# Attention in 64x32 tiles of TensorE, even heads above, odd heads below, with products in the free half

## The chip, the cores and the metric

The kernel runs on one core of one Trainium2 chip. The metric is the device time of one execution in microseconds (us). A core has a matrix engine (TensorE, in the views PE for its matmuls and PEld for its weight loads), a vector engine (VectorE, DVE), a scalar engine (ScalarE, ACT), GpSimd (POOL) and a queue engine that here only issues DMAs (SyncE, SP). The engines run side by side, each through its own instructions in program order, and wait for each other by semaphores. SBUF is the working memory, of 128 partitions; PSUM is the memory into which TensorE writes, eight banks of 128 x 512 fp32 values.

## The reference: what is computed

Four layers of multi-query attention, in which two sets of weights alternate (A, B, A, B), on one sequence of S = 2048 rows of D = 512, with H = 32 query heads of width 16 and one key and one value head for all of them:

```python
q = (x @ wq).reshape(B, S, H, Dh).transpose(0, 2, 1, 3)
k = x @ wk
v = x @ wv
scores = einsum("bhqd,bkd->bhqk", q, k) * Dh ** -0.5
o = einsum("bhqk,bkd->bhqd", softmax(scores), v)
x = x + o.transpose(0, 2, 1, 3).reshape(B, S, H * Dh) @ wo
```

where the `x` on the right of the first three lines is the layer norm of the layer's input. All is fp32. Of a layer the scores are the bulk: 32 x 2048 x 2048 exponentials, 4 x 134 million in all.

## The kernel before, in words

**Tiling.** Queries are cut into NB = 4 blocks of 512, the 32 heads into NM = 4 groups of 8. A *pair* (lines 486 on) is a layer, a block and a group: 64 pairs. The 8 heads of a pair are taken in two halves of four, even and odd (`odd`). For one half and one chunk of 128 keys, a *unit*, `scores` (line 566) makes two score tiles `st` of 128 keys x 1024 (two heads x 512 queries) in PSUM. Each is two matmuls side by side: a weight of 64 rows x 128 keys (`kop`) and 512 moving columns of queries (`qt`), one in rows 0 to 63 of the array and one in rows 64 to 127. The 64 rows hold 16 dimensions four times, since key and query are each kept as a sum of two fp16 numbers. Three `st` tiles (NST = 3, six banks) take turns.

**Exponentials.** ScalarE turns an `st` into probabilities `pt` in SBUF (line 598, fp32, eight buffers). No maximum is subtracted; a check of ranges sets a flag, and a general path that is not taken here would do the work again. For 274 of the 4,096 tiles (letter V) VectorE does it instead, in `v_exp` (line 605): one operation that reads PSUM (line 609), two on the bits of the result (611, 613) and four of a polynomial (614 to 617), each reading what the one before wrote.

**Probabilities times values.** `pv` (line 619) is four matmuls of a unit (line 636) with fp32 weights of 128 keys x 32 columns (`vop`: 16 of values, 16 of ones, so that numerators and denominators come together) and 512 moving columns of `pt`, side by side in the four column strips of the array. An fp32 matmul is two passes in the records. They add up in a bank `acc` over the 16 chunks. `merge` (line 505) then moves numerators and denominators of even and odd heads from `acc` into two sums (lines 515, 518). For a whole pair come a reciprocal of 512 columns (line 537), a shuffle that brings denominators to their numerators (538), a multiplication (539) and the split into two fp16 parts (540, 541).

**Products.** Queries, keys, values and outputs are fp16 products in three terms (`mm3`, lines 297 to 299: high x high, high x low, low x high), as full 128x128 matmuls of 512 columns: 12 for one tile of 512 columns, and 64 + 16 + 64 such tiles in all. Around them stand layer norm (`normed`, line 311), transposes (338), splits, and squared lengths for the check (414, 416). They run as generators, one piece for each letter M, m or l, in whichever of the two `acc` banks is idle. Query tiles go to DRAM and come back in the layout of `qt` by eight DMAs for each pair (line 454).

**Order.** A string `ORDER` (line 57) fixes the order of everything after the front part: S and V for a score tile (exponential on ScalarE or VectorE), P and Q for `pv` of the first or second waiting unit, M, m and l for background work, v for one operation of a VectorE exponential, d for one of a division. The loop of line 673 walks through it; each engine's program follows. Scores come in runs of two or four, then probabilities, then background, so TensorE goes from one tile shape to another some thousands of times.

Of the kernel before, what the change touches and what calls it, by code (L numbers as in the profile page):

```python
# [31 lines left out]
W = 2  # L32
NST = 3
NPT = 8
# [14 lines left out]
LEAD4 = 0.01353416811725628  # L49
C0, C1, C2, C3 = 37.67975997924805, 23.0539493560791, 12.31057357788086, -0.15702559053897858  # L50
LOG2E = 1.4426950408889634

# [4 lines left out]
ORDER = (  # L57
    "mSSSMMMSSSPPSSMSSPPSSMMSSSPPSSMMSSPSSPPSSSPPSSMMSSSMMSPSSPSSMPSmSPSSPPSSSPmPSMSSPSSPPSSSMPSPSSSPMSSPSSPM"
    "SSPSmSMMSSPSMMSSPSSPSSMPSmSPPSSSPPSSPmSSPMSSPSSMSPSSPPSMSSSPPSSSPMSSPSmSMMMSSSMPSSPSSPPSMSSPmSSPPSSSPPmS"
    "SSMPSSPSSPMSSPSSMSPSSPPSSMSSPPmSSMSSMMSSPMSSPSSPSSMPSmSPPSSVPvSmSSPSPvSSvSmQSQvSQvSSmSQvSVQSSmPvSSvSPSSQ"  # L60
    "mmmQSSSQlvSMvMSvSQvSSMdMSSQQSSSPdPSSPdSdSPdPSVSPvSSvMvSSPvQvSSMvMSSVQvSMSSSPPSvSPvSSQvQvSSSQvQdSSPSSPPSS"
    "VPSvMvSSvSMMvMSSSPvQSvSQdSSdQdPdSSVPSMSvSMvSSvPPvSSSvQvQSSdMMSSSQPSSdPdVSMSPSSSmPvPvSvSQSvSMvMSSQvQVSSMv"
    "MSSSvQvQvSSPSSQvQSvSSQddQdSSPSSPPdSdVSPSvMvSSMSvSPQvSSvMMSSvSQlQddSSQVSPvSSvSPvPSSMvMSSvSQvQSSMVSQvSSvSQ"
    "vPvSSPvSSQvQSVSQvSSvMSSPvPSvSSQvQvSSMSSQQSVSPSSMvSSvPvPSvSSQvQvSSMdMSSSQQSSPdSSdPdPdVSSMvMvSSvSPPvSSvQSv"
    "SMMSSQVSQvSSvSPvPSSPvSSQvQvSSSMMVSQvSSvSQvPvSSPvSSQvQSVSMvMSSSQvPvSSPvSSvQQvSVSQSvMSSPmSSPvQvSSSvMMSSvQQ"
    "vSSdSQQSSMdSSdPdPdSVSPvSvSMSSvPPvSSvQSvSQVSQvSSvSMvMSSPvPSSSQvQvSSMVSQvSSvSQvPvSSPvSSQvQSVSQvSSvSPvPvSSS"
    "vQQvSMSVSQmSSSPPSSSQvQmSvSSvMQSSQvSSQvMSSQSSQvMSSQSdSPPSSPdSSdPdSdMSSPPmSSMVSPvSSvSMvMMSSSPQSSQSvSQvMSSQ"
    "QmvSSVMMSvSSQvPvSSvPSvSQvQSSVQvSMvSvSSPvPSvSMSSQvQSVSPSSSPvPvSvSMvMSSSQvQvSSQdSSQPSSdSPdPddSSMMSVSPmvSSv"
    "SPvPvSSMvSSQvQSVSQvSvSMSSvPPSSSvQQvSSvMSVMSQvSSvSQvPvSSPvSSQvQSVSMvMSSSvQvPSvSPvSSQvQSVSQvSSvSMvMSSPmPSS"
    "SQQSSQvSSvQmQvSSSMQSSPdPSSSPPdSdSMSPSdSPdMSSPSVPvSMSSPSmSMvMvSSQvSSMvMSSQQSSSQvQSVMSQvSSSlvPvPSvSQvSSMvQ"  # L70
    "SVSQvSvSSPvPvSSMvSSQvQSVSPSSMvSSvPvPSvSSQvQvSSMSSQdQSSPSSPdSdSPddPSVSPvSvSMvMSvSSPvQSvSQSVMSvMSSSQvPSSPv"
    "SSQvQvSSSMvMVSQvSSvSQvPvSSPvSSQvQSVSQvSSvMvMSSSPvPSSvQSvSQQSVSPSSMvSSvPvPSvSSQvQvSSQdSSQSSPdPdSSdMdMSVSP"
    "vSSvMSSPvPSvSQvSSQvQSSVQvSMSSvPmSSPvQSvSSMvMSSQvQSVSQvSvSSPvPvSSMvSSQvQSVSQvSvSMSSvPPvSSvQSvSMMSSQVSQvSS"
    "vSPPSvSPvSSQvQSvSSQdQSSPSSdPdPddSSVMMSSvSPmvPvSSvMMSSvSQvQSVSQvSSvSMvMSSPvPSSSQvQvSSMVSQvSSvSQvPvSSPvSSQ"
    "vQSVSQvSSvMSSvPPvSSvSQvQSVSQvSSvSMvMSSPvPmSSSQQSSQSvSQvQmSSVQSvMSSPSSvPvSQvSSQvSSvQMSSQSdSPPSMSSPSSdPPSd"
    "SVPSMSSPvSmvSMvMSvSQvSSQvQSdSdMVSQvSSvSPvPvSSMSSQQSSvSQvQSSVQvSMSSPlmSSPSQlSQvSvSSQvSSmQvSSQvSVQmSSSvPvS"
    "PvSSvQmSQSvSSQvSSmQdPSSPSSPmlmSSPSSPlSdSdMdMdSSPPSVSPvSSvMvSSPvQvSSMSSQvQSSMVSQvSSvSPvPvSSMvSSQvQSVSQvSv"
    "SPvSSMvMSSPSSQvQSvSSQdQSSPSSPdPddSSdSMMVSPvSSvSPvPvSSQvSSMvMSSQSSQPSVSPvSvSPSSMvMSSvPSvSQvQVSSMvMSSSQvQv"
    "SSPvSSvQQvSSVQSvMSSQmvSvSPvPSvSSQvQSSQSSPddddddddddddddddddddPSSSPPSSMMSSPSSPPSSSMMSSPPSSMMSSSPPSSPSSMMS"
    "SPmSSPPSSMSSPPSSMSSPPSSMSSPPSSMSSPmPSSMSSPPSSSPPSSMSSPMSSPSMSSPmSSPPSSSPPmSSSMPSSPMSSSPPSSPMSSSPPSSMPSSS"  # L80
    "mMMMSSSMPSSPSSPSPMSVSPmvSSvSPvPSSQmSSQvSSvQSvSmSPSSPPmSSSPSPSPmSSPdSPSSPmSSPdSmmSPSSVPlvSSvSMvMSvSMMSSPS"
    "SQvQvSSSQdQddSSdPSSPPdSVSPSvMvSSvSPvQSvSMSvSQdQdSdSSPPSVSPvSvSSMvMSPSSSQvQvSSMvSSQQSVSPvSvSSPvPvSSMvSSQv"
    "QSVSQvSvSMvMSSSPvPSvSQSvSQQSVSPSSMvSSvPvPSvSMSvSQvQSdSSQQSSMdSdSPddPSVSPvSvSMSSPvPvSSQvSSQvQSSVQvSMSSvPm"
    "SSPvQSvSSMvMSSQvQSVSQvSvSSPvPvSSMvSSQvQSVSQvSvSMSSvPPvSSvQSvSMMSSQVSQvSSvSPPSvSPvSSQvQSvSSQdQSSPSSdPdPdd"
    "SSVMMSSvSPmvPvSSvMMSSvSQvQSVSQvSSvSMvMSSPvPSSSQvQvSSMVSQvSSvSQvPvSSPvSSQvQSVSQvSSvMSSvPPvSSvQSvSQVSQvSSv"
    "SMvMSSPvPmSSSQQSSQSvSQvQmSSVQSvMSSPSSvPvMSSQSSQvQvSSSMQSSvQMSSQdSmSPPSSSPPdSdSMddMSSMVSPvSSvSPvPvSSMSSQQ"
    "SSvQSvMSSQQlSSMVSPvSSvSPvPvSSMvSSQvQSVSPSSMvSSvPvPSvSSQvQvSSMSSQdQSSPSSPdPddSVSMMvSvSSPvPvSSQvSSMvMSSQdQ"
    "SVSPvSSvPSSMvMSSvPSvSQvQSSMVSQvSSvSQvPvSSPvSSQvQSVSQvSSvMSSPvPSvSSQvQvSSQSVPSSSPvPvSvSMMvSSQvSSvQQdSSSPP"
    "SdSMdMSSPddSVMSPSvSSPmvPvSSvMMSSvQSvSQQSVSQvSSvPSSPvQvSSSMvMSSQvQSVSQvSvSSPvPvSSMvSSQvQSVSQvSvSMSSvPPvSS"
    "vSQvQSVSQvSSvPSSPvSSMvMSSQlvQvSSSQdQSSPSdSPdPddSVSMMvSvSSPvPvSSMvMSSQSvSQQSVSQvSSvSPvPSSMvMSSvSQvQSSQVSQ"  # L90
    "vSSvSPvPvSSMvMSSSQvQSSMVSQvSSvSQvPvSSPvSSQvQSVSQvSSvPSSMvMSSvPSvSQvQSdSSQQSSPdSdSPddPSVSPvSSvMSSPvQSvSSM"
    "vMSvSQQSVSQvSSvMvMSSSPvPSSQSvSQQvSVSQSvMSSPmvSvSPvQSvSSQvQSSMVSPvSvSMSSvPPvSSvQSvSQVSQvSSvSMvMSSPPSvSSQv"
# [86 lines left out]
def fast_path(ctx, tc, x_in, weights, out, flag):  # L181
# [80 lines left out]
    def load_split(key, w):  # L262
# [3 lines left out]
        for c in range(NC + 2):  # L266
# [8 lines left out]
            if c:  # L275
                yield False
# [564 lines left out]
```

## Time and profile before

| | |
|---|---|
| median of 3 runs | 3643.64 us (3640.91 to 3644.29) |
| profiled execution, first to last instruction (span) | 3639.3 us |
| TensorE busy (matmuls) | 3575.5 us, 26,707 records |
| ScalarE busy | 3552.5 us |
| VectorE busy | 3084.4 us |
| first and last exponential on ScalarE | 36.13 us, 3619.19 us |
| mean granted TensorE clock | 0.996 of full speed |

The profile is of one execution of its own, and its page gives no time for it but the span; the median of the runs is 4.3 us above that span. In the views a group of instructions is given by line, engine, operation, what is written and read with partitions x elements and type, the count, then busy time in us and the mean of one in ns, then the engine's idle time just before and what ended it. A timeline row has start, length, engine and line, and merges like instructions that follow one another (x8). A busy engine need not be at its peak: the records of matmuls overlap, and a record also holds latency.

### The profile page before, as it was taken

Reading aid. Unit: us, or ns where it says so; the run is one execution under the profiler, and the core shown is the slowest. Engines: PE = TensorE matmul, PEld = TensorE weight load, DVE = VectorE, ACT = ScalarE, POOL = GpSimd, SP = SyncE. Lnnn points to the kernel's source line nnn. Section 1 sums busy time; section 2 is a strip of 40 time slices with the busy share of each in tenths; the row PEclk is TensorE's granted clock in tenths of the full one; section 3 lists DMA queues with packets and bytes.
Section 4 is the critical chain, followed back from the end, with each engine's and each line's share of the span. In section 5 each row is a group of like instructions: output and inputs, shape, how many; then the busy total and the mean of one; then the engine's idle time right before and its main releaser. Section 6 shows DMA issues by size and latency. Waiting matters only on the chain.

```text
span 3639.3 us, 63025 instructions
## 1 busy us (share of the span) xinstructions
PE 3575.5 (98%) x26707; PEld 925.5 (25%) x26707; DVE 3084.4 (85%) x3606; ACT 3552.5 (98%) x3828; POOL 116.8 (3%) x122
## 2 busy tenths in 40 slices
PE   7999999999999999999999999999999999999998
PEld 2222222222222222222222222222222222222221
DVE  4598989998578998988958889988986889899988
ACT  6999999999999999999999999999999999999997
POOL 1000000000000000000000000000000000000000
PEclk9999999999999999999999999999999999999999
DMA  2110100000010010101001000010101101010000
GB/s 89 41 53 13 47 11 29 21 30 30 24 50 21 24 36 13 41 19 36 24 30 45 15 29 25 18 42 18 47 7 36 47 16 36 21 36 13 23 20 13
DMA packets 94819, 108.11 MB, mean 30 GB/s; under 512 B 15936, under 2 KB 72256, under 8 KB 94528
## 3 DMA queue, kind: packets, MB, share of 16 engines
q1 hardware_dynamic: 94208, 102.95, 8.8%
q8 instruction: 211, 3.46, 0.4%
q0 software_dynamic: 320, 1.05, 0.1%
q14 instruction: 80, 0.66, 0.1%
HBM read 70.39 MB, written 33.55 MB: 29 GB/s over the span
## 4 chain that ended last, share of the span: by engine, by line
PE 86%; ACT 11%; DVE 2%; DMA 1%; issue 0%; SPq 0%; POOL 0%; ACTq 0%; DVEq 0%; POOLq 0%
PE acc L636 47%; PE st L581 27%; ACT pt L598 10%; PE qps L297 2%; PE ops L297 2%; PE qps L298 1%; PE qps L299 1%; PE ops L299 1%; PE ops L298 1%; ACT dpt L598 1%; PE tps L338 1%; PE kps L297 0%; DVE den L537 0%; PE kps L299 0%; PE kps L298 0%
## 5 line engine op out<-in xcount | busy, mean ns | idle before, releaser
L598 ACT ACTIVATE pt<-st 128x1024 f32<-128x1024 f32 x3548 | 3311.5, 1046 | 41.0 <-PE st L581 30.4
L636 PE MATMUL acc<-pt,vop 128*32 128x512 f32 x14192 | 1799.5, 601 | 0.1
L581 PE MATMUL st<-qt,kop 64*128 64x512 f16 x8192 | 1269.5, 382 | 30.8 <-DMA qt<-qs 9.7
L581 PEld LDWEIGHTS <-kop 64*128 64x128 f16 x8192 | 357.0, 94 | 1581.5 <-issue 1474.1
L636 PEld LDWEIGHTS acc<-pt,vop 128*32 128x32 f32 x14192 | 345.5, 108 | 704.8 <-issue 684.7
L609 DVE TENSOR_SCALAR e<-st 128x1024 int32<-128x1024 f32 x274 | 335.3, 1224 | 199.3 <-PE st L581 194.8
L617 DVE SCALAR_TENSOR_TENSOR dpt<-dpt,e 128x1024 f32<-128x1024 f32 x274 | 339.7, 1240 | 8.5
L615 DVE SCALAR_TENSOR_TENSOR dpt<-dpt,mant 128x1024 f32<-128x1024 f32 x274 | 338.9, 1237 | 7.1
L616 DVE SCALAR_TENSOR_TENSOR dpt<-dpt,mant 128x1024 f32<-128x1024 f32 x274 | 336.9, 1230 | 7.6
L614 DVE SCALAR_TENSOR_TENSOR dpt<-mant 128x1024 f32<-128x1024 f32 x274 | 336.4, 1228 | 0.0
L636 PE MATMUL acc<-dpt,vop 128*32 128x512 f32 x2192 | 290.8, 602 | 0.0
L598 ACT ACTIVATE dpt<-st 128x1024 f32<-128x1024 f32 x274 | 282.9, 1033 | 5.0 <-ACT pt L598 4.3
L537 DVE RECIPROCAL den<-den 128x512 f32<-128x512 f32 (+1 forms) x76 | 215.9, 2841 | 0.4
L613 DVE TENSOR_SCALAR e<-e 128x1024 int32<-128x1024 int32 x274 | 193.6, 707 | 7.9
L611 DVE TENSOR_SCALAR mant<-e 128x1024 int32<-128x1024 int32 x274 | 189.8, 693 | 8.2
L436 DVE SCALAR_TENSOR_TENSOR xt<-ops,xt 128x512 f32<-128x512 f32 x140 | 96.4, 688 | 79.0 <-PE ops L299 78.1
L403 POOL TENSOR_TENSOR sq<-qs 128x512 bf16<-128x512 f16 x64 | 66.8, 1043 | 1611.6 <-DVE qs L400 1611.6
L518 DVE SCALAR_TENSOR_TENSOR num<-acc,half,num 128x512 f32<-128x512 f32 x92 | 69.0, 750 | 56.6 <-PE acc L636 55.7
L297 PE MATMUL ops<-wo,ot 128*128 128x512 f16 x252 | 97.4, 386 | 3.7 <-DVE xt L436 3.7
L297 PE MATMUL qps<-xnT,wq 128*128 128x512 f16 x256 | 99.1, 387 | 1.4 <-DVE wq L269 0.7
L298 PE MATMUL qps<-xnT,wq 128*128 128x512 f16 x256 | 97.4, 380 | 0.6 <-DVE xnT L342 0.6
L299 PE MATMUL qps<-xnT,wq 128*128 128x512 f16 x256 | 97.3, 380 | 0.4 <-DVE wq L270 0.4
(99 smaller groups left out, 1383.2 us busy)
## 6 DMA issues: line engine op xcount, KB each, us to landing
qt<-qs SPq DMA_DIRECT2D x624, 64.0 KB, 2.2
qs<-qs SPq DMA_DIRECT2D x64, 256.0 KB, 2.2
xs<-xt SPq DMA_DIRECT2D x48, 256.0 KB, 2.0
xt<-xs SPq DMA_DIRECT2D x48, 256.0 KB, 3.4
xt<-in_A_x_dram SPq DMA_DIRECT2D x32, 256.0 KB, 3.5
out_dram<-xt SPq DMA_DIRECT2D x16, 256.0 KB, 2.1
wst<-in_A_wo_dram SPq DMA_DIRECT2D x8, 256.0 KB, 2.7
wst<-in_B_wq_dram SPq DMA_DIRECT2D x8, 256.0 KB, 2.7
```

Of the source, the lines that this page charges most:

```text
L297: PE.matmul(ps, a[0], b[0], start=first, stop=False)
L537: lambda c=c: V.reciprocal(den[:, c], den[:, c]),
L581: PE.matmul(st[:, k * 512:(k + 1) * 512], kop[l % 2][c // 4][r, (c % 4) * P:(c % 4 + 1) * P], qt[pr][r, 2 * half + odd], start=True, stop= ...
L598: e = nc.scalar.activation(pt, st, AF.Exp, scale=SCALE / UP / UP).ins
L609: V.tensor_scalar(e, st, SCALE / UP / UP * LOG2E * 2.0 ** 23, 127 * 2.0 ** 23, ALU.mult, ALU.add)
L611: lambda: V.tensor_scalar(mant.bitcast(I32), e, 0x7FFFFF, 0x3F800000, ALU.bitwise_and, ALU.bitwise_or),
L613: lambda: V.tensor_scalar(e, e, 0x7F800000, None, ALU.bitwise_and),
L614: lambda: V.scalar_tensor_tensor(p, mant, C3, mant, ALU.add, ALU.mult),
L615: lambda: V.scalar_tensor_tensor(p, p, C2, mant, ALU.add, ALU.mult),
L616: lambda: V.scalar_tensor_tensor(p, p, C1, mant, ALU.add, ALU.mult),
L617: lambda: V.scalar_tensor_tensor(p, p, C0, e.bitcast(F32), ALU.add, ALU.mult)])
L636: PE.matmul(acc[s][32 * j:32 * j + 32, :], v[l % 2][c // 4][:, c % 4, 16 * odd:16 * odd + 32], p_of[u, j % 2][:, (j // 2) * 512:(j // 2 + ...
```

## The change

Nearly all of the fast path is written anew; the arithmetic is the same but for the constants of the VectorE exponential.

- **One tile shape.** Scores, probabilities and most products run as 64x32 tiles: `both` issues up to two lists of operations, one for rows 0 to 63 and one for rows 64 to 127, each operation being four matmuls in the four column strips. A score tile (`score`) is now 64 keys x all 8 heads of the pair: upper rows and lower rows of the array give columns 0 to 511 and 512 to 1023, and the even heads come out on partitions 0 to 63, the odd ones on 64 to 127. `pv(0)` takes even heads in the upper rows, `pv(1)` odd heads in the lower, each with 64 keys x 32 weights and 256 columns, into a bank of its own (`acc[0]`, `acc[1]`).
- **Products in the other half.** A full product becomes 24 half products of 64 rows x (4 x 32) columns. A table `STEPS` gives each letter its upper and lower operation: a is even and odd probabilities, b two half products above and odd probabilities below, c the reverse, and so on; V is half a score tile for VectorE. All products use one bank, `beside`. F (transposes, squared lengths) and P (full products in the front and at the end) keep other shapes.
- **Buffers.** Two score tiles instead of three, a bank `by_v` for scores that VectorE reads, `beside`, and two for sums; 16 probability buffers instead of 8.
- **VectorE exponentials.** 378 instead of 274; two chains can be open, letters 0 and 1, and one is taken up to 24 tiles ahead of the others. The first operation is done in two halves of 512 columns (letter I).
- **Sums and divisions.** An `acc` is copied or added as a whole (letter G, 170 times instead of 312 merges). For a division DMAs gather the 8 rows of denominators into a tile of 128 x 32, VectorE inverts that, and DMAs by way of DRAM spread the result over 16 partitions for each head. The last pair keeps the old way.
- **Outputs** of a block start when all four groups of it are divided, instead of group by group. Splits of weights and norms are single operations (letter X), Y is a copy of one column, weights are loaded from SP's queue. The order string is new (14,484 letters, 3,718 of them S, 756 with half a score tile for VectorE).

The diff, cut to its core:

```diff
-W = 2
-NST = 3
-NPT = 8
+NST = 2
+NPT = 16
+AHEAD = 24
...
+STEPS = {"S": "SS", "a": "EO", "b": "NO", "c": "EN", "d": "MO", "e": "EM", "f": "VO", "g": "EV",
+         "h": "WO", "i": "EW", "j": "VM", "k": "MV", "l": "E-", "m": "-O", "n": "N-", "o": "-N",
+         "p": "M-", "q": "-M", "r": "V-", "s": "-V"}
...
-    vop = [[one.tile([P, 4, 48], F32, name=f"vop{i}_{b}") for b in range(NB)] for i in range(2)]
+    vop = [[one.tile([P, 8, 32], F32, name=f"vop{i}_{b}") for b in range(NB)] for i in range(2)]
...
+    def both(ops):
+        turn[0] += 1
+        for n in range(max(map(len, ops))):
+            for r in range(2):
+                if n >= len(ops[r]):
+                    continue
+                bank, o, w, x, start, stop = ops[r][n]
...
+                h = slice(64 * r, 64 * r + 64)
+                for j in range(4):
+                    PE.matmul(o[32 * j:32 * j + 32], w[j][h], x[j][h], start=start, stop=stop,
+                              skip_group_check=True, tile_position=(64 * r, 32 * j))
...
+    def moving(n, r):
+        g, c, h = halves[n]
...
+        k = kop[l % 2][c // 8][:, c % 8 * 64:c % 8 * 64 + 64]
+        q = qt[groups[g][0]]
+        return (cols(k) * 2, [q[:, 2 * h], q[:, 2 * h], q[:, 2 * h + 1], q[:, 2 * h + 1]], True, True)
...
-        for k in range(W):
-            r = slice(64 * k, 64 * k + 64)
-            PE.matmul(st[:, k * 512:(k + 1) * 512],
-                      kop[l % 2][c // 4][r, (c % 4) * P:(c % 4 + 1) * P],
-                      qt[pr][r, 2 * half + odd], start=True, stop=True)
+        both([[(("st", s, r), st[s][:, 512 * r:512 * r + 512]) + moving(n, r)] for r in range(2)])
...
-        for j in range(4):
-            v = vop4 if u in split and j % 2 == 0 else vop
-            PE.matmul(acc[s][32 * j:32 * j + 32, :],
-                      v[l % 2][c // 4][:, c % 4, 16 * odd:16 * odd + 32],
-                      p_of[u, j % 2][:, (j // 2) * 512:(j // 2 + 1) * 512],
+        v = vop[l % 2][c // 8][:, c % 8]
+        cs = slice(256 * n, 256 * n + 256)
+        x = [pts[:, i[j % 2], (j // 2) * 512 + 256 * n:(j // 2) * 512 + 256 * n + 256]
+             for j in range(4)]
...
+        return ("acc", odd), acc[odd][:, cs], [v] * 4, x, (c, n) == (2 * c0, 0), last
...
+    def step(what):
+        ops = [[], []]
+        for r, w in enumerate(STEPS[what]):
+            if w in "EO":
+                ops[r].append(pv(r))
+            if w in "VW":
+                ops[r].append(score_v(r))
+            for _ in range({"N": 2, "M": 1, "W": 1}.get(w, 0)):
+                ops[r].append(work.next_pe().step(r))
+        both(ops)
...
+    def divide(pr):
...
+        for j in range(4):
+            for odd, t in ((0, ev[32 * j + 16:32 * j + 17]), (1, od[32 * j:32 * j + 1])):
+                h = 32 * j + 16 * odd
+                SP.dma_start(den[h:h + 16], t.rearrange("o (p q) -> o p q", p=16))
...
+        def invert():
+            V.reciprocal(den, den)
+            SP.dma_start(rs.rearrange("h (p q) -> (h p) q", p=16), den)
+            for j in range(4):
+                SP.dma_start(ev[32 * j + 16:32 * j + 32], od[32 * j + 16:32 * j + 32])
...
+        def spread():
+            r.append(one.tile([P, BQ], F32, name="rec"))
+            for h in range(2 * NM):
+                SP.dma_start(r[0][16 * h:16 * h + 16], rs[h:h + 1].to_broadcast([16, BQ]))
```

1159 lines of the change are left out of this document (701 added, 458 removed).

## The prediction

> **What bounds the kernel now.** I read the page's busy shares first, then the chain that ended last, then the groups by line.
>
> ```profile
> span 3639.3 us, 63025 instructions
> PE 3575.5 (98%) x26707; PEld 925.5 (25%) x26707; DVE 3084.4 (85%) x3606; ACT 3552.5 (98%) x3828; POOL 116.8 (3%) x122
> PE 86%; ACT 11%; DVE 2%; DMA 1%; issue 0%; SPq 0%; POOL 0%; ACTq 0%; DVEq 0%; POOLq 0%
> L598 ACT ACTIVATE pt<-st 128x1024 f32<-128x1024 f32 x3548 | 3311.5, 1046 | 41.0 <-PE st L581 30.4
> L636 PE MATMUL acc<-pt,vop 128*32 128x512 f32 x14192 | 1799.5, 601 | 0.1
> L581 PE MATMUL st<-qt,kop 64*128 64x512 f16 x8192 | 1269.5, 382 | 30.8 <-DMA qt<-qs 9.7
> ```
>
> Two engines are at 98%, and the chain says which one leads: 86% of it is TensorE. Busy time doesn't say what TensorE does with it. The chain in order of time and TensorE's timeline do:
>
> ```profile
> 2000.54 1.85 PE acc L636 x16
> 2002.39 0.76 PE st L581 x6
> 2003.15 0.99 PE acc L636 x8
> 2004.14 0.32 PE st L581 x2
> ...
> 2012.05 0.39 PE L297 MATMUL ops<-wo,ot 128*128 128x512 f16 x1
> 2012.27 0.38 PE L298 MATMUL ops<-wo,ot 128*128 128x512 f16 x1
> 2012.49 0.38 PE L299 MATMUL ops<-wo,ot 128*128 128x512 f16 x1
> ```
>
> Full products start 0.22 us apart (0.216 over five), so 512 fp16 columns stream in 0.216. A score run of two matmuls (one pair, side by side) takes 0.32 and one of six 0.76: 0.22 for each pair and 0.10 once. A probability-value run of 8 takes 0.99 and of 16 1.85: 0.43 for each pass of four, and 0.13 once. So every run of one tile shape pays **0.10 to 0.13 us when the shape changes** (64x128 for scores, 128x32 for probabilities, 128x128 for products). In the order string score letters stand next to probability letters 2,710 times and background letters next to either 1,209 times, of which I take 800 to issue matmuls: 2,710 x 0.115 + 800 x 0.10 = 392 us. Streaming itself is 4,096 pairs x 0.216 = 885, 4,096 fours x 0.43 = 1,761, 144 products of 12 x 0.216 = 373, the small ones about 40: 3,059. With 36 before the first exponential and 20 after the last (rows below) TensorE needs 3,507.
>
> ```profile
> 36.13 1.02 ACT L598 ACTIVATE pt<-st 128x1024 f32<-128x1024 f32 x1 [11.16 <-PE st L581]
> 3611.76 7.43 ACT L598 ACTIVATE pt<-st 128x1024 f32<-128x1024 f32 x8
> ```
>
> Eight exponentials in 7.43 us with 1.03 for one give a spacing of 0.91. ScalarE needs 3,822 x 0.91 + 56 = 3,534. The span is 105 above that: the price of two engines that wait for each other in a fixed order. Times here are spans of the profiled execution; the median of the runs, 3643.64, is 4.3 above it.
>
> **The change part by part.** *Shapes.* Scores, probabilities and most products become 64x32 tiles, four across and two high. Streamed columns stay: a score tile is 8 matmuls of 512 columns at once (0.216), a probability step is two passes of 256 fp32 columns in each half (0.43), and a product takes half the array and so twice as many steps, in the half that a probability step leaves free. Counting the new string by its table: 3,718 S x 0.216 = 803; 4,913 steps with a probability pass (a to i, l, m) x 0.43 = 2,113; 1,154 short steps (j, k, p, q, r, s) x 0.216 = 249; 15 long ones 6. The 93 F (transposes, squared lengths) keep other shapes; I take 0.65 for each, a few short matmuls between two changes: 60 (twice that would still lie inside TensorE's slack below). Sum 3,234; the changes left are these excursions instead of some 3,500. Whether a change of type alone costs as much (scores are fp16, probabilities fp32) one place shows:
>
> ```profile
> 68.61 0.40 PE L414 MATMUL gps<-sq,bones 128*32 128x512 bf16 x4
> 68.84 0.38 PE L416 MATMUL gps<-ksq,bones 128*32 128x512 bf16 x1
> 68.84 1.23 PE L636 MATMUL acc<-pt,vop 128*32 128x512 f32 x8
> ```
>
> From bf16 to fp32 in the same 128x32 tiles the next pass starts 0.23 us after the last, no 0.1 added; and while one column tile still ran line 416, the others went on, so unequal halves needn't wait for each other. I take zero for a type change (less than nothing is excluded, since columns can't stream faster; the other end, 0.115, is a rival below).
>
> *Front and end.* The front is the same work in nearly the same order: 36, give or take 5. The end loses the early output products: all 12 products of four rows come behind the last division, through one bank, instead of 3. That is 36 more at 0.216, and these are not hidden: +8, and four combinations instead of two merges +1, waits for the one bank +3. So 32 instead of 20. TensorE needs 3,234 + 68 = **3,302**.
>
> *ScalarE.* 104 fewer exponentials: 3,718 x 0.91 + 68 = **3,451**.
>
> *VectorE* gets those 104 (274 to 378), so every one of its rows counts.
>
> ```profile
> L609 DVE TENSOR_SCALAR e<-st 128x1024 int32<-128x1024 f32 x274 | 335.3, 1224 | 199.3 <-PE st L581 194.8
> L617 DVE SCALAR_TENSOR_TENSOR dpt<-dpt,e 128x1024 f32<-128x1024 f32 x274 | 339.7, 1240 | 8.5
> L613 DVE TENSOR_SCALAR e<-e 128x1024 int32<-128x1024 int32 x274 | 193.6, 707 | 7.9
> L400 DVE TENSOR_SCALAR qs<-qps 128x512 f16<-128x512 f32 x64 | 43.7, 683 | 34.7 <-PE qps L299 19.8 <-issue 14.3
> L537 DVE RECIPROCAL den<-den 128x512 f32<-128x512 f32 x60 | 200.8, 3346 | 0.2
> L537 DVE RECIPROCAL den<-den 128x128 f32<-128x128 f32 x16 | 15.2, 948 | 0.1
> L538 DVE STREAM_SHUFFLE tmp<-den 128x512 f32<-128x512 f32 x60 | 44.2, 737 | 0.0
> L541 DVE TENSOR_TENSOR ot<-num,ot 128x512 f16<-128x512 f32 x60 | 41.9, 698 | 1.9
> L518 DVE SCALAR_TENSOR_TENSOR num<-acc,half,num 128x512 f32<-128x512 f32 x92 | 69.0, 750 | 56.6 <-PE acc L636 55.7
> ```
>
> Means aren't spacings on this engine:
>
> ```profile
> 274.22 1.22 DVE L615 SCALAR_TENSOR_TENSOR dpt<-dpt,mant 128x1024 f32<-128x1024 f32 x1
> 275.48 1.22 DVE L616 SCALAR_TENSOR_TENSOR dpt<-dpt,mant 128x1024 f32<-128x1024 f32 x1
> 276.62 0.68 DVE L436 SCALAR_TENSOR_TENSOR xt<-ops,xt 128x512 f32<-128x512 f32 x1
> 277.22 1.22 DVE L617 SCALAR_TENSOR_TENSOR dpt<-dpt,e 128x1024 f32<-128x1024 f32 x1
> ```
>
> Line 616 needs 615's result and starts 1.26 after it; 436 needs nothing of 616 and starts 1.14 after it, before it has ended. A stranger in between saves 0.12. The new order works two chains in turn and puts other work between, so that only 251 of the 2,268 chain operations that would pay it follow their own predecessor. Per exponential: two halves from PSUM 2 x 0.60, two integer steps 2 x 0.61, four 4 x 1.14: 6.98. 378 x 6.98 + 251 x 0.12 = 2,668. The sums give back: 312 merges of 0.745 become 170 evacuations of 0.66 (232 to 112). The reciprocal falls from 512 columns to 32 (by its two rows 6.2 ns a column, so about 0.3) and the shuffle goes; a division is now 388 in all (216 of it reciprocals, four more operations of 0.44 to 0.74), then 126. Of the 3,084 busy that leaves 393 for norms, splits and copies beside 2,071 of exponentials; a few copies go: 382. The 135 touches of one column 13. Sum **3,301**, and 45 at both ends where it has little: 3,346.
>
> *Queues.* Each of 63 divisions adds 21 DMAs to SP's queue (8 gather sums, 1 stores reciprocals, 4 move rows, 8 spread them), and weight loads move there from POOL's.
>
> ```profile
> 1999.80 2.30 SPq L454 DMA_DIRECT2D qt<-qs  x5
> qt<-qs SPq DMA_DIRECT2D x624, 64.0 KB, 2.2
> ```
>
> At 0.46 an issue that is 1,323 x 0.46 = 609 us more of SP's queue, under a fifth of the span; some wait for a landing (2.2) and hold the query loads behind them. A pair of head groups lasts some 54 us, and loads are issued ahead, which hides it: I take zero, and up to 60 in all if the cover goes.
>
> *New waits.* Two score tiles instead of three: the S that waits for an exponential holds back all TensorE steps behind it. A score for VectorE waits until its one bank is read; a product waits until VectorE has read the bank of the last one; each holds the queue in the same way. After the end of an exponential 0.22 of streaming and some 0.16 of latency (0.38 in the rows less 0.22) fit into the 0.91 of the other tile, unless a 0.43 step stands in front. Bounded by nothing and by 135 (now 105, a third more for the third engine); I take 60, since TensorE now has 150 to spare under ScalarE where it had 27.
>
> Sum: 3,451 + 60 = 3,511 of span, 4 around it: **3515 us**.
>
> **The rivals.** *The order locks three engines.* Priced as above and counted over any 200 S, TensorE needs 167 to 180, ScalarE 182, VectorE 175 to 184: no engine can absorb another's delay. Waits of 150 instead of 60 give 3,600. For it: now too 105 us are lost with only two engines tied. Against: 16 probability buffers instead of 8.
>
> *VectorE becomes the bound* (the other side). Place: the chains of the 378 exponentials. If the strangers between don't overlap, each operation costs its mean and 0.03: 756 x 0.71 + 756 x 0.74 + 1,512 x 1.26 + 633 = 3,634, with both ends **3,700**. It decides from a mean spacing of 1.22 for the long ones on; the rows above say 1.14 beside a stranger, so little speaks for it but the missing slack.
>
> *TensorE is handed too many instructions.* 64x32 tiles take 111,000 matmuls and as many loads, 223,000 instead of 53,414. It decides at (3,643 - 68) / 223,000 = 16 ns each.
>
> ```profile
> 148.62 0.38 PE L581 MATMUL st<-qt,kop 64*128 64x512 f16 x2
> 149.04 0.19 PEld L636 LDWEIGHTS acc<-pt,vop 128*32 128x32 f32 x8 [0.53 <-PE st L581]
> 149.07 0.64 PE L636 MATMUL acc<-pt,vop 128*32 128x512 f32 x4
> ...
> 2009.65 1.92 PE L636 MATMUL acc<-pt,vop 128*32 128x512 f32 x16
> 2011.51 0.61 PE L581 MATMUL st<-qt,kop 64*128 64x512 f16 x4
> ```
>
> After a wait 8 loads (each 0.11) and 4 matmuls start within 0.08 us: 7 ns each. The longest dense stretch has 32 in 1.86, 58 ns, but there the array sets the pace. Between 7 and 58 I take the burst; at 18 ns the time would be 4,080. [...]
>
> *The change doesn't do what it says:* a change of type drains the array too. S alternates with other steps some 7,300 times: + 840, 4,140. Only the place at 68.8 us speaks against it.
>
> **How the numbers follow.** Forecast 0.62 (3440 to 3600), locked order up to the old time 0.14, within 0.2% (about what a measurement of this kernel can tell from no change) 0.04, VectorE bound 0.07, instructions 0.08, type change 0.05. Low end: no waits and a spacing just under 0.91 (0.905). High end: 3660, which holds the first three, 0.80. Faster 0.76, same 0.04, slower 0.20.
>
> **What would show it.** ScalarE stays at 96% or more with about 3,718 exponentials; TensorE's share of the chain falls and ScalarE's grows; score and probability steps start 0.22 and 0.43 apart with no 0.1 between; VectorE is busy for 95% or more; the end takes about 32 us. Wrong would be: steps of eight matmuls at 0.3 or more (instructions or type), VectorE's long operations at 1.26 (its bound), or ScalarE idle before scores by several hundred us (locked order).

## The result, and the profile after

| | before | changed |
|---|---|---|
| median of 4 runs | 3643.09 us (3640.91 to 3644.29) | 4017.83 us (4014.05 to 4022.31) |
| ratio, 95% interval | | 1.103 (1.101 to 1.105) |
| span of the profiled execution | 3639.3 us | 4020.5 us |
| mean granted TensorE clock | 0.996 | 0.953 |

The forecast was 3515 us, faster, with a range of 3440 to 3660. The kernel became 10% slower. The page of the changed kernel, its busy shares, the chain that ended last by engine, and the group of ScalarE's exponentials:

```profile
span 4020.5 us, 236136 instructions
...
PE 3565.0 (89%) x111943; PEld 2278.3 (57%) x111943; DVE 3326.8 (83%) x4449; ACT 3457.8 (86%) x3724; POOL 151.9 (4%) x110
...
DVE 31%; PE 31%; SPq 16%; ACT 11%; DMA 7%; issue 3%; DVEq 0%; POOL 0%; ACTq 0%
...
L752 ACT ACTIVATE pt<-st 128x1024 f32<-128x1024 f32 x3718 | 3453.6, 1081 | 508.3 <-PE st L469 501.8
```

No engine is near 98% now, so no engine's work alone is the bound. The chain says what came in: 16% of it is SP's queue and 7% transfers, which had been 0 and 1%. ScalarE waits 502 us for scores, but that is only who was waited for last. The waits of the changed kernel (engine and line, what it waited for, then us in total, times, longest) show where it starts:

```profile
ACT pt L752 <- PE st L469: 501.8, 276, 10.6
DVE sum L917 <- DMA rec<-rs: 236.0, 60, 10.0
DVE den L899 <- DMA den<-sum: 201.2, 51, 6.1
PE by_v L469 <- DVE e L781: 165.5, 65, 9.7
...
PE by_v L469 <- DMA qt<-qs: 37.2, 16, 7.7
```

Read from the bottom of a dependence up: ScalarE waits for TensorE, TensorE (by_v, the scores that VectorE reads) waits for VectorE, and VectorE waits for transfers at the reciprocal (den, line 899) and at the multiply (line 917) of the 63 divisions, 201.2 + 236.0 = **437 us**. One division in SP's queue and on VectorE (start, length):

```profile
2008.99 6.62 SPq L894 DMA_DIRECT2D den<-sum  x8
2017.31 0.34 SPq L900 DMA_DIRECT2D rs<-den  x1
2017.70 2.42 SPq L902 DMA_DIRECT2D sum<-sum  x4
2020.16 4.54 SPq L907 DMA_DIRECT2D rec<-rs  x8
```

```profile
2007.68 1.28 DVE L871 COPY sum<-acc 128x512 f32<-128x512 f32 x2
...
2010.73 1.23 DVE L790 SCALAR_TENSOR_TENSOR pt<-pt,mant 128x1024 f32<-128x1024 f32 x1
2016.92 0.35 DVE L899 RECIPROCAL den<-den 128x32 f32<-128x32 f32 x1 [4.97 <-DMA den<-sum]
...
2022.46 0.69 DVE L781 TENSOR_SCALAR e<-by_v 128x512 int32<-128x512 f32 x1
2026.39 0.69 DVE L917 TENSOR_TENSOR sum<-sum,rec 128x512 f32<-128x512 f32 x1 [3.25 <-DMA rec<-rs]
```

The sums are in SBUF at 2008.96. The eight gathers take 6.62 us to issue, the last lands 1.3 later; VectorE got to its reciprocal at 2011.96 and stood 4.97 us. From its end (2017.27) to the multiply lie 9.1 us: a store, four moves, eight spreads that start only behind them, and a landing. In the written order the reciprocal stands 3 to 5 score steps behind the second evacuation in 52 of the 63 divisions (4 in 37 of them), and the multiply 6 to 13 behind the reciprocal, 7.4 in the mean. With ScalarE's spacing of 0.92 us a step that is 3.7 us for four steps and about 7 us.

### The profile page after: what moved, and what is told of

Read it like the earlier page. It is cut to its first block, busy times and chain, and to the rows that moved or that the text cites. A ratio compares the mean times of both kernels' runs of the same rounds, so it can differ in the third digit from the quotient of the medians.

```text
span 4020.5 us, 236136 instructions
## 1 busy us (share of the span) xinstructions
PE 3565.0 (89%) x111943; PEld 2278.3 (57%) x111943; DVE 3326.8 (83%) x4449; ACT 3457.8 (86%) x3724; POOL 151.9 (4%) x110
## 4 chain that ended last, share of the span: by engine, by line
DVE 31%; PE 31%; SPq 16%; ACT 11%; DMA 7%; issue 3%; DVEq 0%; POOL 0%; ACTq 0%
PE acc L469 15%; DVE pt L790 15%; ACT pt L752 11%; PE st L469 8%; SPq L894 6%; SPq L907 5%; PE beside L469 5%; DVE e L781 5%; SPq L902 3%; DMA rec<-rs 3%; DMA den<-sum 3%; DVE e L798 2%; DVE mant L796 2%; SPq L719 2%; PE by_v L469 1%
## 5 line engine op out<-in xcount | busy, mean ns | idle before, releaser
L469 PE MATMUL acc<-pt,vop 64*32 64x256 f32 x65536 | 2981.2, 386 | 33.3 <-DVE pt L790 19.9
L469 PE MATMUL st<-qt,kop 64*32 64x512 f16 x29744 | 1818.5, 390 | 39.8 <-ACT pt L752 21.9
L469 PEld LDWEIGHTS acc<-pt,vop 64*32 64x32 f32 x65536 | 1566.2, 108 | 419.7 <-issue 41.0
L469 PEld LDWEIGHTS <-kop 64*32 64x32 f16 x32768 | 799.1, 92 | 967.3 <-issue 655.1
L790 DVE SCALAR_TENSOR_TENSOR pt<-pt,mant 128x1024 f32<-128x1024 f32 x756 | 925.5, 1224 | 3.9
L781 DVE TENSOR_SCALAR e<-by_v 128x512 int32<-128x512 f32 x756 | 519.0, 687 | 76.2 <-PE by_v L469 49.9
L469 PE MATMUL beside<-xnT,wq 64*32 64x512 f16 x5952 | 481.1, 395 | 84.0 <-DVE seen L856 45.3
L469 PE MATMUL beside<-wo,ot 64*32 64x512 f16 x5760 | 451.8, 385 | 25.3 <-DVE seen L856 11.1
L790 DVE SCALAR_TENSOR_TENSOR pt<-pt,e 128x1024 f32<-128x1024 f32 x378 | 461.5, 1221 | 0.9
L790 DVE SCALAR_TENSOR_TENSOR pt<-mant 128x1024 f32<-128x1024 f32 x378 | 460.5, 1218 | 0.1
L917 DVE TENSOR_TENSOR sum<-sum,rec 128x512 f32<-128x512 f32 x63 | 43.6, 692 | 236.0 <-DMA rec<-rs 236.0
L899 DVE RECIPROCAL den<-den 128x32 f32<-128x32 f32 x63 | 22.1, 351 | 201.2 <-DMA den<-sum 201.2
```

Of the source, the lines that this page charges most:

```text
L469: PE.matmul(o[32 * j:32 * j + 32], w[j][h], x[j][h], start=start, stop=stop, skip_group_check=True, tile_position=(64 * r, 32 * j))
L781: V.tensor_scalar(e[:, 512 * r:512 * r + 512], by_v, SCALE / UP / UP * LOG2E * 2.0 ** 23, LEAD, ALU.mult, ALU.add)
L790: n = V.scalar_tensor_tensor(p, a, c, b, ALU.add, ALU.mult).ins
```

## The experiments

Theory A: VectorE stands at the divisions because the transfers take longer than the written order leaves for them, and everything behind it in the fixed order waits too. Against it: the order alone locks three engines (B), SP's queue is too full for the query loads (C), VectorE's own work is the bound (D).

| kernel | us | ratio to before (95%) | wait at reciprocals + multiplies, us |
|---|---|---|---|
| changed | 4017.83 | 1.103 (1.101 to 1.105) | 201.2 + 236.0 |
| e1: VectorE waits for no transfer | 3612.92, one run | | 0 |
| e2: no transfers for the divisions | 3575.66, one run | | 0 |
| e3: later letters | 3707.62 | 1.0185 (1.0168 to 1.0202) | 32.9 + 27.6 |
| e4: one spread for eight | 3902.86 | 1.0708 (1.0691 to 1.0726) | 205.0 + 88.7 |
| e5: nine transfers for 21 | 3715.32 | 1.0203 (1.0182 to 1.0224) | 0.7 + 122.5 |
| e6: nine transfers, later letters | 3636.64 | 0.9979 (0.9966 to 0.9992) | 0 + 15.3 |
| e7: division on VectorE | 3918.21 | 1.0755 (1.0737 to 1.0772) | 0 |
| e8: e6, moves on GpSimd's queue | 3627.99 | 0.9950 (0.9936 to 0.9964) | 0 + 1.7 |
| e9: letters half as late | 3826.96, one run | | 49.6 + 111.9 |
| e10: 21 transfers on GpSimd's queue | 3942.85, one run | | 150.8 + 207.0 |
| e11: e8, all nine on GpSimd's queue | 3640.36 | 0.9990 (0.9981 to 0.9999) | 0.6 + 13.0 |

### Without the waits, and without the transfers (e1, e2)

```diff
-                SP.dma_start(den[h:h + 16], t.rearrange("o (p q) -> o p q", p=16))
+                SP.dma_start(den[h:h + 16], ones[h:h + 16])
...
-            V.reciprocal(den, den)
+            V.reciprocal(inv32, ones)
...
-                SP.dma_start(ev[32 * j + 16:32 * j + 32], od[32 * j + 16:32 * j + 32])
+                SP.dma_start(r[0][32 * j + 16:32 * j + 32], od[32 * j + 16:32 * j + 32])
...
-        divs.extend([invert, spread, lambda: V.tensor_tensor(ev, ev, r[0], ALU.mult), parts, rest])
+        divs.extend([invert, spread, lambda: V.tensor_tensor(ev, ev, ones[:, 0:1].to_broadcast([P, BQ]), ALU.mult), parts, rest])
```

That is e1; e2 has the same VectorE operations and none of the `dma_start` lines of `divide`. Both leave the division out: `ones` is a tile of constants, and no engine reads what the reciprocal or the transfers write.

> Leaves out the division itself: VectorE's five operations of each division are still there, at their places and with their shapes, but read a constant, so that nothing on VectorE waits for a gather or a spread; the 63 x 21 transfers are all still issued, into tiles that nobody reads. Theory A (VectorE stands at the divisions for the transfers, 236.0 us at the multiplies and 201.2 at the reciprocals, and all that is behind it in the fixed order waits with it): 4,018 - 437 = 3,580 us, between 3,540 and 3,640, the granted clock back at 0.99, and the two waits gone. Rival B (the fixed order of three engines costs the time whatever stands in it, so what VectorE does not wait for here it waits for elsewhere): above 3,850. Rival C (SyncE's queue, 1,323 more transfers, holds up the queries' loads): no change, 3,950 or more, since all the transfers are still there. Rival D (VectorE's own work is the bound): about 3,700.

> Leaves out the division and the merging of the odd heads' rows: as the kernel in which VectorE reads a constant, and the 21 transfers of each division are gone as well. Theory A: the transfers alone cost next to nothing once nobody waits for them, so within 40 us (the 37.2 us that TensorE waits for query tiles) of the kernel that keeps them, about 3,560. Rival C (the queue): this one gains what that one does not, 3,600 beside 3,950. Rival B: above 3,850, as there. The difference between the two kernels prices the queue.

e1 took 3612.92 us and e2 3575.66, one run each. Their pages (the first fence is e1, the second e2), each with the busy shares and the group of ScalarE's exponentials:

```profile
PE 3464.6 (96%) x111943; PEld 2218.1 (61%) x111943; DVE 3326.2 (92%) x4450; ACT 3440.4 (95%) x3724; POOL 152.2 (4%) x110
...
L755 ACT ACTIVATE pt<-st 128x1024 f32<-128x1024 f32 x3718 | 3436.2, 1089 | 116.0 <-PE st L472 109.9
```

```profile
PE 3448.6 (96%) x111943; PEld 2211.8 (62%) x111943; DVE 3325.4 (93%) x4450; ACT 3439.0 (96%) x3724; POOL 152.2 (4%) x110
...
L755 ACT ACTIVATE pt<-st 128x1024 f32<-128x1024 f32 x3718 | 3434.8, 1090 | 81.0 <-PE st L472 74.7
```

VectorE does the same 3,326 us of work as in the changed kernel, and all transfers of e1 are still issued. Only the waits are gone, and with them 405 us; 392 of ScalarE's 502 went too. So A holds, and B at 3,850, C at 3,950 and D at 3,700 are out. In e1 SP's queue, too, no longer waits for VectorE's sums and reciprocals (182 and 50 us in the changed kernel), so the 405 us hold whatever that cost. The transfers as such cost the difference of the two, 37 us. It isn't the 37.2 us at the query tiles, which the expectation of e2 had taken for it: they are mostly still there without any of these transfers (e1 first, then e2).

```profile
PE by_v L472 <- DMA qt<-qs: 36.4, 17, 6.9
```

```profile
PE by_v L472 <- DMA qt<-qs: 27.3, 17, 4.0
```

### The distance (e3, e9)

Only letters D in the order string move. One division of e3 (evacuation G, a score step S, then reciprocal, spread, multiply and two parts as D):

```diff
-SGlISaXaXSa0SaaXSaDXSa0aSaXS0FaXD0SaX0SaaXS0aSaXaXDSi0SaaISaD0ShbISbDkSbIp0Sa0Sa0aScj0ScqISc0Sca1Si0SaaYISa0Sa0aSa0rSapISa0SbaX
+SGlISaXaXSa0SaaXSaXSa0aSaXS0FaX0SaX0SaaXS0aSaXaXSDi0SDaaISa0ShbISbkSbIp0Sa0Sa0aScj0ScqISc0Sca1Si0SaaYISDa0Sa0aSDa0rSapISDa0SbaX
```

> Only the written order is changed: the letters of 60 of the 63 divisions are moved later, the reciprocal at least 12 score steps behind the second evacuation (4 before) and the multiply at least 14 behind the reciprocal (8 before), less where the outputs follow at once; three stay as they are. All computation is there. A score step lasts about 0.9 us, so the transfers have 10.8 and 12.6 us, against 9.2 (8.0 to the landing and a little) and 9.4 seen. Theory A: nearly all of the 437 us goes, 3,590 to 3,640, under the 3,643 of the kernel before. Rival B (locked order): 3,900 or more, since no work and no distance of the three engines' loops is changed. Rival C (queue): no change, 3,980 to 4,020, since all transfers stay. Rival E (the late divisions meet the outputs, which then wait): 3,750 to 3,850.

e3 took 3707.62 us: 310 less than the changed kernel by moving letters alone, yet 68 more than A's upper end. The 437 us of waits fell to 60.5:

```profile
DVE e L781 <- PE by_v L469: 75.3, 93, 7.5
...
DVE den L899 <- DMA den<-sum: 32.9, 9, 4.9
...
DVE sum L917 <- DMA rec<-rs: 27.6, 11, 5.3
```

B (3,900 or more) and C (3,980 or more) are out here too, and E (3,750 or more) by 42 us. What is left lies in 20 places; 5 reciprocals still stand 4 or 5 steps behind their sums, and 6 multiplies 6 to 11 behind their reciprocals. Moving isn't free either: VectorE waits 75.3 us for its own scores here, 49.9 in the changed kernel.

> All 21 transfers as in the changed kernel, and the letters moved half as far as in the kernel with only the order changed: the reciprocal 8 score steps behind the second evacuation (4 before, 12 there), the multiply 11 behind the reciprocal (8 before, 14 there), in 58 of 63 divisions. All computation is there. At 0.92 us a step that is 7.4 and 10.1 us against 9.2 (8.0 to the landing, and what holds the queue) and 9.4 needed. Theory A: the multiplies wait no more and the reciprocals 63 x 1 to 2 us, so 100 us at the reciprocals and 20 at the multiplies: 3,708 + 60 = 3,770. Rival B (order): no more than 50 us under 4,018, since the distance is not what counts.

e9 took 3826.96 us (one run): half the distance brings more than half of the gain, but 57 us less of it than A said. The reciprocals wait 49.6 us, half of what was expected, but the multiplies 111.9 instead of 20. Both terms of that estimate were off. In the divisions whose multiply waits, VectorE comes to it 9.0 us behind the reciprocal in the median, not the 10.1 that 11 steps of 0.92 would give, and the transfers in between take 10.9 us, not 9.4. SP's queue at the longest of these waits, 6.0 us:

```profile
2104.92 5.52 SPq L894 DMA_DIRECT2D den<-sum  x8
2110.54 5.59 SPq L719 DMA_DIRECT2D qt<-qs  x8
2116.23 0.38 SPq L900 DMA_DIRECT2D rs<-den  x1
...
2119.84 4.94 SPq L907 DMA_DIRECT2D rec<-rs  x8
```

A query load of 5.6 us stands between a gather and its store, which goes out 3.5 us after VectorE's reciprocal has ended (2112.75). So the chain has no fixed length on a shared queue. But only 8 of the 63 divisions of e9 have such a load between gather and spread, as in the changed kernel; it isn't what makes most of the 48 multiplies wait.

### Fewer transfers (e4, e5)

```diff
-            for h in range(2 * NM):
-                SP.dma_start(r[0][16 * h:16 * h + 16], rs[h:h + 1].to_broadcast([16, BQ]))
+            SP.dma_start(r[0], rs.unsqueeze(1).to_broadcast([2 * NM, 16, BQ]))
```

That is e4; e5 has it too, and:

```diff
-        for j in range(4):
-            for odd, t in ((0, ev[32 * j + 16:32 * j + 17]), (1, od[32 * j:32 * j + 1])):
-                h = 32 * j + 16 * odd
-                SP.dma_start(den[h:h + 16], t.rearrange("o (p q) -> o p q", p=16))
+        SP.dma_start(den[0:64], ev[16:P:32].rearrange("j (p q) -> j p q", p=16))
+        SP.dma_start(den[64:P], od[0:P:32].rearrange("j (p q) -> j p q", p=16))
...
-            SP.dma_start(rs.rearrange("h (p q) -> (h p) q", p=16), den)
+            for o in range(2):
+                SP.dma_start(rs.rearrange("(j o) q -> o j q", o=2)[o], den[64 * o:64 * o + 64])
```

> The eight transfers that spread a division's reciprocals over the rows become one with the same 128 rows of 2 KB; all else, the order too, is as in the changed kernel. All computation is there. Theory A: the last of the eight is issued 7 x 0.42 = 2.9 us behind the first, and VectorE stood 236.0 / 63 = 3.75 us at each multiply: if the one lands as the last of eight did, 63 x 2.9 = 183 us go, 3,835; if the one with eight times the bytes lands 1 us later, 120 go, 3,900. Rival B and D: no change, 4,018, since the wait only moves. Rival C (queue): 441 x 0.42 = 185 us less of the queue, a gain as in A, but at the query tiles and not at the multiplies, whose 236.0 us would stay.

> Order as in the changed kernel; of the 21 transfers of a division 9 are left: two gathers of four rows each for eight of one row, two stores for one, four moves as before, one spread for eight. All computation is there. Theory A: on top of the kernel with one spread (3,903, where 205.0 us were left at the reciprocals and 88.7 at the multiplies) the last gather is issued 6 x 0.59 = 3.5 us earlier, against waits of 205.0 / 50 = 4.1 us: 50 x 3.5 = 175 us less, 3,730, if a gather of four rows lands as one of one row does. Rival F (the landing goes by the number of pieces of 128 bytes, not by the number of transfers): the wait at the reciprocals stays near 200 and the time at 3,900. Rival B (locked order): 3,850, for half of what goes comes back elsewhere.

e4 took 3902.86 us, A's second figure, and e5 3715.32, 15 under A's 3,730. The first fence is e4, the second e5:

```profile
DVE den L899 <- DMA den<-sum: 205.0, 50, 6.5
...
DVE sum L916 <- DMA rec<-rs: 88.7, 40, 7.9
```

```profile
L915 DVE TENSOR_TENSOR sum<-sum,rec 128x512 f32<-128x512 f32 x63 | 43.5, 691 | 135.3 <-DMA rec<-rs 122.5 <-issue 11.4 <-DMA sum<-sum 1.2
...
L897 DVE RECIPROCAL den<-den 128x32 f32<-128x32 f32 x63 | 21.6, 344 | 0.8 <-DMA den<-sum 0.7
```

Each edit takes most of the wait that it aims at: 147 of 236 us at the multiplies with one spread, and nearly all of 205 at the reciprocals with two gathers (of which 34 come back at the multiplies, 88.7 to 122.5). The number of issues counted, not the bytes or the pieces: the same 128 pieces landed in time (F is out). So is B's 3,850.

### A queue of its own (e10)

```diff
-                SP.dma_start(den[h:h + 16], t.rearrange("o (p q) -> o p q", p=16))
+                G.dma_start(den[h:h + 16], t.rearrange("o (p q) -> o p q", p=16))
```

The other transfers of `divide` are changed in the same way.

> The changed kernel with one edit: all 21 transfers of a division go through GpSimd's queue, and SyncE's keeps query tiles, weights and rows as in the kernel before. Order and count as changed; all computation is there. Theory A1 (the wait is the chain's own length: 8 issues of 0.54 on GpSimd against 0.59 on SyncE and a landing of 2.3 for the gather, store, four moves and 8 issues for the spread): the waits at the divisions fall by a tenth from 437, and the query tiles' 37: 3,960 to 4,000. Theory A2 (query loads of 4 to 5 us that stand between the steps of a division on the shared queue make half of the wait): 3,780 to 3,830. Rival H (GpSimd's own waits hold the transfers): above 4,018.

e10 took 3942.85 us (one run), 75 less than the changed kernel.

```profile
DVE sum L917 <- DMA rec<-rs: 207.0, 57, 8.0
...
DVE den L899 <- DMA den<-sum: 150.8, 52, 5.3
```

Of 437 us 358 stay without any query load in the way. So most of the wait is the chain's own length against the distance (A1, which gave 3,960 or more, 17 us above the run; A2 gave 3,830 or less). The 79 us that went are about a fifth. They are not the shared queue alone: GpSimd issues the gathers faster (0.52 us each, 0.59 on SP's queue) and the spreads slower (0.51 and 0.42), and its own work may hold transfers. No run separates these.

### The division back on VectorE (e7)

```diff
-        divs.extend([invert, spread, lambda: V.tensor_tensor(ev, ev, r[0], ALU.mult), parts, rest])
+        divs.append(first)
+        divs.append(lambda: V.scalar_tensor_tensor(d[0], od, lo, d[0], ALU.mult, ALU.add))
+        divs.append(lambda: V.tensor_scalar(ev, ev, lo, None, ALU.mult))
+        divs.append(lambda: V.scalar_tensor_tensor(ev, od, hi, ev, ALU.mult, ALU.add))
+        for c in range(0, BQ, P):
+            divs.append(lambda c=c: V.reciprocal(d[0][:, c:c + P], d[0][:, c:c + P]))
+        divs.extend([turn_back, parts, rest])
```

> One part of the change undone: the division is done by VectorE alone, as in the kernel before (two masks, two combinations, the reciprocal in four pieces of 128 columns, shuffle, multiply, two parts), its letters spread over the score steps that follow, with no transfer at all; tiles, exponentials and the rest of the order as changed. All computation is there. VectorE gets 63 x (4 x 0.69 + 4 x 0.95 + 0.73 - 0.35) = 437 us more work than the 3,325 of the kernel without transfers: 3,762. Theory A: no waits for transfers, but VectorE is the bound: 3,762 + 45 at both ends + up to 60 of waits, 3,800 to 3,870; so the packing is needed, and what it cost was only where it stood. Rival G (VectorE stands 248 us idle in the kernel without transfers and takes half of the work there): 3,690 to 3,760. Rival B: about 4,018, as the 437 us of waits are replaced by 437 of work.

e7 took 3918.21 us; it lies between A and B.

```profile
PE 3546.8 (91%) x111943; PEld 2263.3 (58%) x111943; DVE 3688.8 (94%) x5016; ACT 3470.5 (89%) x3724; POOL 151.0 (4%) x110
...
L755 ACT ACTIVATE pt<-st 128x1024 f32<-128x1024 f32 x3718 | 3466.3, 1069 | 393.4 <-PE st L472 382.1
```

`first` starts with the masked denominators, `turn_back` is the shuffle and the multiply. VectorE has 363 us more work than in e2 (437 were expected) and the time is 343 longer, though VectorE stood 248 us idle in e2: in this order its idle time takes up nearly nothing. Why not, these runs don't settle; B is right in that work costs here as much as waits do. The packing is worth 3918 - 3628 = 290 us to these tiles, once its transfers have time (against e8, below); another placing of e7's letters wasn't tried.

### Both edits together (e6, e8, e11)

e6 is e5 with later letters (most reciprocals 10 score steps behind the sums, most multiplies 11 behind the reciprocals). e8 also moves the multiplies to 14 steps behind the reciprocals, and:

```diff
-                SP.dma_start(ev[32 * j + 16:32 * j + 32], od[32 * j + 16:32 * j + 32])
+                G.dma_start(ev[32 * j + 16:32 * j + 32], od[32 * j + 16:32 * j + 32])
```

In e11 the gathers, stores and spread go through `G` too.

> The nine transfers, and the division's letters later: 58 of 63 with the reciprocal 10 score steps behind the second evacuation and the multiply 11 behind the reciprocal, two a little nearer, three as they were. All computation is there. Theory A: no division but the three waits; under the kernel with only the order changed (3,708) by its 61 us left at the divisions and some 20 of the queue: 3,600 to 3,640, which would be under the 3,643 of the kernel before and between the two kernels without waits (3,576 and 3,613). Rival B (what is left at 3,708 is not the transfers but the later divisions that meet other work): 3,680 to 3,710.

> The kernel with nine transfers and later letters, with two edits: the four moves of a division go through GpSimd's queue instead of SyncE's, and 58 of 63 multiplies stand 14 score steps behind their reciprocal instead of 11. All computation is there. Theory A: the 15.3 us left at the multiplies go, and 252 x 0.59 = 149 us less of SyncE's queue give some 10 of the 36.6 us at the query tiles: 3,637 - 25 = 3,612, 3,600 to 3,625. Rival H (GpSimd's own waits, up to 30 us for a squared length, hold the moves, and VectorE waits for them at the multiply): waits of 100 us or more at the multiplies, 3,700. Rival B (the later letters meet other work): 3,640 to 3,660.

> The kernel with nine transfers, later letters and moves on GpSimd's queue, and now its gathers, stores and spread there too. All computation is there. No division waits there any more (1.8 us), so only the query tiles' 33.6 us can shrink: under A2, where the divisions' transfers hold query loads on the shared queue, 3,628 - 20 = 3,608; under A1 nothing, 3,628; under rival H the spread comes late and the multiplies wait, 3,640 or more.

e6 took 3636.64 us, e8 3627.99, e11 3640.36. Two waits of e8, and then two of e11:

```profile
DVE e L781 <- PE by_v L469: 77.6, 95, 9.8
...
PE by_v L469 <- DMA qt<-qs: 33.6, 21, 5.9
```

```profile
DVE sum L915 <- DMA rec<-rs: 13.0, 6, 6.1
...
DVE xn L365 <- POOL rstd L358: 11.9, 7, 3.5
```

e6 lies in A's range, at its upper end. All three are back at the time of the kernel before, and under it by 0.1 to 0.5%. e8 is the best of the kernels that compute everything, by little: 16 us under the kernel before. It fell short of A's 3,600 to 3,625 by 3 us. In e11 the multiplies wait for the spreads again (13.0 us, 1.7 in e8) and the layer norm waits for GpSimd (11.9), and 12 us are lost (H, which gave 3,640 or more). The 52 us between e8 and e2 are not settled. VectorE waits 77.6 us for its scores in e8 and 49.1 in e2, TensorE 33.6 and 27.3 for query tiles; what belongs to the transfers that are left and what to the moved letters wasn't separated.

## Why the prediction was wrong, step by step

**The step that failed is "Queues"**: the 1,323 transfers of the divisions, taken at zero and at most 60. It priced them as load on SP's queue, which is right as far as it goes: 37 us (e1 less e2, one run each). It missed that they are a chain at whose links VectorE, which runs in order, waits (4.97 us at the reciprocal above: line 790's next operation, whose input was there from 2011.96 on, started at 2017.19). That cost 4018 - 3613 = **405 us**. None of the rivals named it either: what was given to a slower kernel stood for VectorE's work, the instructions and the type change. The sum could have been made from the rows that stood there, 0.46 us an issue and 2.2 a landing: a gather needs 8 x 0.46 + 2.2 = 5.9 us, and the order gives 4 steps, 3.7; reciprocal, store, landing, eight spreads, landing need 0.35 + 0.46 + 2.2 + 5.9 = 8.9 (the four moves are issued while the store lands), and the order gives about 7. The 2.2 us missing at the 52 reciprocals and 1.9 at the 63 multiplies are 234 us: 3515 + 234 = 3,749, slower than before. No run splits the rest. The waits came to 437 us and not 234, since the transfers took longer than these rows say: a gather's issue 0.59 us in the median (0.83 at 2009 us), and from reciprocal to multiply 10.1 us in the median where VectorE waits. Query loads lie between in 8 divisions. Another 62 us are in ScalarE's spacing and the small waits, below.

**TensorE's steps: right** (but for the sum, which adds up to 3,231 and not 3,234; TensorE had 150 us to spare). The chain in order of time, at a place without a division:

```profile
2074.03 0.22 PE st L469 x8
2074.24 0.43 PE acc L469 x16
2074.68 0.22 PE beside L469 x4
2074.89 0.22 PE st L469 x8
2075.11 0.86 PE acc L469 x32
```

Score steps are 0.22 and probability steps 0.43, with nothing between them where fp16 meets fp32. (Other score steps of that stretch take 0.32 or 0.33. There four steps in turn, 0.22, 0.43, 0.33 and 0.86, add up to 1.84, twice ScalarE's 0.92, so TensorE most likely waits for ScalarE.) So the rival of the type change is out, and that of the instructions: a score step is eight matmuls and eight loads in 0.22 us, 13.8 ns each, and all of e2 has 223,886 of them in 3,574 us, 16.0 ns each.

**ScalarE: the spacing was too low.** Two rows of its timeline, a dense stretch and the last exponentials:

```profile
2042.15 88.42 ACT L752 ACTIVATE pt<-st 128x1024 f32<-128x1024 f32 x96 [1.18 <-PE st L469]
```

```profile
3969.04 18.56 ACT L752 ACTIVATE pt<-st 128x1024 f32<-128x1024 f32 x20
```

Over 95 steps (88.42 - 1.03) / 95 = 0.92, where the prediction took 0.91 (0.914 before rounding) from eight at the end of the kernel: 3,718 x 0.01 = 37 us too little. The end, 4020.5 - 3987.6 = 32.9 us, was right (32); its parts weren't told apart. The first exponential starts at 32.5 us, within the 36, give or take 5.

**VectorE's work: right**, 3,326 busy against 3,301; it isn't the bound where its waits are gone (e2: 93%).

**Waits of 60:** e2 has 3574 - (3,718 x 0.92 + 68) = 85 us (under the bound of 105 and a third more, which is 140 and not 135). So without the transfers the forecast would have stood: 3,576 against 3,515, 37 us more by the spacing and 25 by the waits, and inside the range.

One of the signs given misled: ScalarE idle before scores by several hundred us was to mean the locked order. It was there (502 us), but 392 of it went with the transfers' waits. Here the order only carried a wait of one engine to the others.

## What to carry to other kernels

When an in-order engine's work is replaced by transfers, don't price the transfers by the load of their queue: write down the chain (issues one after the other, landing, next link) and hold it against the time that the written order leaves in front of each instruction that waits. Many small transfers in a link cost their issues in latency (6.62 us for the eight gathers above), so put them into one, and move the waiting instruction back until the chain fits; do both, since here neither alone came back to the old time (e3 and e5: 3,708 and 3,715). And read a wait table down to the engine that waits for something that isn't an engine: the largest row (502 us) was only the echo.

## What was not expected of the hardware

TensorE's clock fell from 1.00 to 0.50 behind a wait, and the price went on after it. The windows of the changed kernel around the division above (us, then each engine's busy time, then the granted clock, the DMA share and GB/s), and its matmuls:

```profile
2013.00:2016.00 3.00, 3.00 (x112) 1.93 (x93) 0.00 (x0) 3.00 (x5) 0.00 (x0) 1.00 0.05 8
2016.00:2020.00 4.00, 1.29 (x32) 0.64 (x32) 3.08 (x5) 1.67 (x2) 0.00 (x0) 0.86 0.10 21
2020.00:2024.00 4.00, 3.33 (x84) 1.79 (x75) 3.11 (x5) 2.05 (x2) 0.00 (x0) 0.72 0.22 56
2024.00:2028.00 4.00, 3.94 (x140) 2.31 (x127) 1.61 (x4) 3.86 (x5) 0.00 (x0) 1.00 0.16 34
```

```profile
2015.89 0.41 PE L469 MATMUL st<-qt,kop 64*32 64x512 f16 x8
2019.00 0.62 PE L469 MATMUL by_v<-qt,kop 64*32 64x512 f16 x4 [2.71 <-DVE e L781]
...
2021.51 0.67 PE L469 MATMUL st<-qt,kop 64*32 64x512 f16 x4
...
2025.22 0.41 PE L469 MATMUL st<-qt,kop 64*32 64x512 f16 x8
```

After 2.71 us of standing the same 512 columns take 0.67 instead of 0.41 us, for some three us. In windows of half a microsecond the granted clock is 1.00 up to 2018.5, 0.86 in the next, 0.50 from 2019.0 to 2022.0, then 0.73 and 1.00 again: half speed for about 3.4 us, from some 2.6 us after the last matmul on. Over the kernel the granted clock is 0.953 with 437 us of waits, 0.963 in e10, 0.971 in e9, 0.984 in e3 and 0.994 in e2; it is 0.972 in e7, where no division waits for a transfer and TensorE stands 116.6 us for VectorE's reads of its scores (by_v), so the clock is lower there without those transfers. How much of the 405 us the clock made wasn't separated.
